# Regrouping the tokens of the expert stage from ragged per-batch blocks into one row of 1024-token blocks

## The chip, the cores and the metric

The kernel runs on one core of a Trainium2 chip. The metric is device time in microseconds (us) of one launch. The engines are PE (TensorE, matrix products), DVE (VectorE), ACT (ScalarE), POOL (GpSimd) and SP (SyncE, whose queue issues nearly all DMAs here). Each engine runs its own instructions strictly in program order and waits on semaphores for the others; the queue of SP does the same.

## The reference

There are 4 sequences of 3008 tokens. The first layer is a linear-algebra attention, the second a gated feed-forward block (called "experts" below) on all 12032 tokens:

```
scores = (z @ z^T) / S;  attn = max(scores, 0)**2;  x = u * (attn @ v)      # per sequence, S = 3008
xn = x / sqrt(mean(x*x) + 1e-6) * rms_g                                      # per token, 256 features
out = (silu(xn @ w_gate) * (xn @ w_val)) @ w_out                             # 256 -> 1536 -> 256
```

Each float32 operand is split into a high and a low part, and every product is three matmuls (high by high, high by low, low by high) of 128x128 weights on up to 512 columns.

## The kernel before

Attention works through the tokens of each sequence in three pairs of chunks: 1024, 1024 and 960 tokens. That makes 12 attention stages, A0 to A11, of 24 key blocks each. The expert layer takes the same 12 groups of tokens, M0 to M11: a group is cut in two halves of n columns (512, or 480 for the short third group of each sequence), and a seven-product scheme makes gate and value of both halves from seven split operands.

An expert stage runs 12 units (class Unit, one for each 128 hidden features). A unit issues 21 matmuls of n columns for the seven products and 12 more for the output product (`y`), 33 in all. Weights `wu` are loaded three units ahead. The program order is A0, A1, A2, M0, A3, M1, A4, M2, ... M8, A11, M9, M10, M11: the expert stage p comes right after attention stage p + 2.

Between attention and experts x goes through DRAM: `emit_gate` (L615) multiplies the attention result by u on DVE and writes it to a DRAM tile `xg`; it runs for the first chunk at the end of the first unit of the next expert stage and for the second chunk in its second unit, since the last three steps of an attention stage are carried over (`pend`). `load_x` (L626) fetches the 1024 or 960 columns back into `ux`; `norm_jobs` (L634) then makes 23 jobs of them: squares (ACT), add, transpose, reduce (DVE), all twice; one small matmul with `fold_sb` (L670) that sums over partitions; 13 tiny DVE instructions for the inverse root; two transposes back, four multiplications (L706) and four subtractions (L721). Seven split jobs (L753, L758) follow.

Where these jobs go is decided before anything is issued. `hook(phase, slot)` runs the jobs of a slot in the middle of the stage's own work; an expert unit f has the slots 3f, 3f + 1 and 3f + 2, so a stage has 36. The class Beside (L986) keeps a budget for every slot: 0.75 for DVE, and 1.35 for ACT in every third slot alone (slots 2, 5, ... 35). `put` goes through a list of jobs in order, gives each the first slot from the last one on that has room for its cost, and if no slot has room, the one with most room left from there on; the next job never goes to an earlier slot. In the stages M0, M3 and M6 `plan_batch` (L1057) puts the loads and splits of the next sequence's keys and values first: 18 casts of cost 0.6 on ACT. These three stages have one more particularity (`late_jobs`, L887): their slot 3f + 2 runs behind the unit's last DVE product and before its last three matmuls.

In this kernel the norm of group p stands in the following places. For p = 3, 6, 9 and for p = 5, 8 all of it lies beside expert stage M(p-1), with the load in the attention stage ahead. For p = 4, 7, 10 (`p % NP == 1`) the first 13 jobs are in attention stage A(p+1), and the other ten in M(p-1) from slot 1 on. The groups 0, 1, 2 and 11 have places of their own.

Of the kernel before, what the change touches and what calls it, by code (L numbers as in the profile page):

```python
# [8 lines left out]
F32 = mybir.dt.float32  # L9
# [10 lines left out]
P = 128  # L20
CH = 512
BLK = 32
# [8 lines left out]
def kernel(  # L31
# [13 lines left out]
    nc = tc.nc  # L45
    D, NT = uT.shape
# [3 lines left out]
    ND = D // P  # L50
    NF = DFF // P
    NK = -(-S // P)
    NC = -(-S // CH)
# [3 lines left out]
    NP = NC // 2  # L57
    PAIR = 2 * CH
    NPAIR = batch * NP
    NU = NF  # L60
    assert NC % 2 == 0 and NK % 4 == 0

    LA = 2
    LAG = 3
# [11 lines left out]
    dram = ctx.enter_context(tc.tile_pool(name="dram", bufs=1, space=bass.MemoryType.DRAM))  # L76

    def f32(ap):
        return ap.bitcast(F32)

    def where(p):

        b, j = divmod(p, NP)
        return b, 2 * j, b * S + j * PAIR, min(PAIR, S - j * PAIR)

    def width(c):
        return min(CH, S - c * CH)

    front = const.tile([P, FRONT], F32, name="front")
    woh = const.tile([P, NF, D], F32R, name="woh")  # L90
# [7 lines left out]
    def at(phase, slot, fn):  # L98
        jobs[phase, slot].append(fn)
# [182 lines left out]
    def prep_mov(p, k):  # L282
        b, c0, t0, n2 = where(p)
        c = c0 + k
        n = width(c)
        tiles = {}

# [32 lines left out]
    def prep_stat(b, c, shared=None):  # L320
        t0 = c * CH
        n = width(c)
        m = n + TAIL if n < CH else n
        lo = slice(DQK, P)
        tiles = shared if shared is not None else {}

        def load():
            raw = tiles["raw"] = new_raw("batch" if b else "start")
            nc.sync.dma_start(out=raw[:, :n], in_=zT2[:, b * S + t0:b * S + t0 + n])
            if n < m:  # L330
                nc.sync.dma_start(out=raw[:, n:m], in_=zT2[:, (b + 1) * S - TAIL:(b + 1) * S])

        def one():
            z = zst[b, c] = keep.tile([P, CH], F32R, tag=f"zst{c}", name=f"zst{c}")
            nc.scalar.copy(z[:, :m], tiles["raw"][:, :m])

        def two():
            raw, z = tiles["raw"], zst[b, c]
            nc.vector.tensor_tensor(z[lo, :m], raw[lo, :m], f32(z[lo, :m]), op=ALU.subtract)

        return load, one, two
# [255 lines left out]
    xg = {}  # L597
# [16 lines left out]

    def emit_gate(p, k):  # L615

        n = width(where(p)[1] + k)
        if p and p not in xg:
            xg[p] = dram.tile([ND, P, PAIR], F32, tag=f"xg{p}", name=f"xg{p}")
        for d in range(ND):  # L620
            x = us.pop((p, k, d))
            nc.vector.tensor_tensor(x[:, :n], acc[k, d][:, :n], x[:, :n], op=ALU.mult)
            if p:
                nc.sync.dma_start(out=xg[p][d, :, k * CH:k * CH + n], in_=x[:, :n])

    def load_x(p):  # L626
        n2 = where(p)[3]
        for d in range(ND):
            t = ux[p, d] = work.tile([P, PAIR], F32, tag=f"ux{d}", name=f"ux{d}")
            nc.sync.dma_start(out=t[:, :n2], in_=xg[p][d, :, :n2])  # L630
# [1 line left out]
    xsplit = {}  # L632

    def norm_jobs(p):  # L634
        n2 = where(p)[3]
        ns = [min(CH, n2 - k * CH) for k in range(2)]
        nb = n2 // BLK
        q = {}
# [1 line left out]
        m, y, w, pp = (small[:, k, :nb] for k in range(4))  # L640
        x = [ux[p, d] for d in range(ND)]
# [68 lines left out]
        n = n2 // 2  # L710
# [27 lines left out]
    ORDER = [A11, A12, S1, S2, S3, A22, S4]  # L738

    def split_jobs(p):  # L740
        n = where(p)[3] // 2
        last = p == NPAIR - 2

        def one(o):
            def high():
                val = xsplit[p, "values"][o]
                if last:
                    hi = keep.tile([P, CH], F32R, tag=f"vh{o}", name="xh")
                    lo = keep.tile([P, CH], F32R, tag=f"vl{o}", name="xl")
                else:  # L750
                    hi = moving.tile([P, CH], F32R, tag=f"xh{o}", name="xh")
                    lo = moving.tile([P, CH], F32R, tag=f"xl{o}", name="xl")
                nc.scalar.copy(hi[:, :n], val)  # L753
                xsplit[p, o] = (hi, lo)

            def low():
                hi, lo = xsplit[p, o]
                nc.vector.tensor_tensor(lo[:, :n], xsplit[p, "values"][o], f32(hi[:, :n]), op=ALU.subtract)  # L758

            return high, low  # L760

        return [one(o) for o in ORDER]
# [20 lines left out]
    class Unit:  # L783
        def __init__(self, p, f):
            self.p, self.f = p, f
            self.n = where(p)[3] // 2

        def product(self, ps, o, start, stop):
            wh, wl = units[self.p, self.f]
# [22 lines left out]
        def y(self, h):  # L812
            p, f, n = self.p, self.f, self.n
            if f == 0:
                for d in range(ND):
                    acc[h, d] = ps_a.tile([P, CH], F32, tag=f"acc{h}{d}", name="py")
            hi, lo = self.h[h]
            for d in range(ND):
                ds = slice(d * P, (d + 1) * P)
                nc.tensor.matmul(acc[h, d][:, :n], woh[:, f, ds], hi[:, :n], start=(f == 0), stop=False)  # L820
                nc.tensor.matmul(acc[h, d][:, :n], wol[:, f, ds], hi[:, :n], start=False, stop=False)  # L821
            for d in range(ND):
                ds = slice(d * P, (d + 1) * P)
                nc.tensor.matmul(acc[h, d][:, :n], woh[:, f, ds], lo[:, :n], start=False, stop=(f == NF - 1))  # L824
            if f == NF - 1:
                t0 = where(p)[2] + h * n
                for d in range(ND):
                    if p == NPAIR - 1 and h == d == 1:
                        out = work.tile([P, CH], F32, tag="T", name="y", bufs=6)
                    else:  # L830
                        out = work.tile([P, CH], F32, tag="out", name="y", bufs=3)
                    if d == 0:
                        nc.scalar.copy(out[:, :n], acc[h, d][:, :n])
                    else:
                        nc.vector.tensor_copy(out[:, :n], acc[h, d][:, :n])  # L835
                    nc.sync.dma_start(out=outT[d * P:(d + 1) * P, t0:t0 + n], in_=out[:, :n])
# [123 lines left out]
    def norms(p):  # L960
        if ("n", p) not in made:
            made["n", p] = norm_jobs(p)
        return made["n", p]
# [12 lines left out]
    def norm_plan(p):  # L976

        kinds = "addd addd tgggg ddd ddd dddd".replace(" ", "")
        cost = {"a": 1.3, "d": 0.7, "t": 0.0, "g": 0.7}
        out = []  # L980
        for i, k in enumerate(kinds):
            gap = 3 if i == 8 else 2 if i == 9 else 0
            out.append(("a" if k == "a" else "d", cost[k], gap, lambda i=i: whole(norms(p)[i])()))
        return out
# [24 lines left out]
    for p in range(NPAIR):  # L1009
        b, c0 = where(p)[:2]  # L1010
        ph = ("A", p)
        m = beside[p] = Beside(p)
# [33 lines left out]
    def plan_splits(p, phase, slots):  # L1046
        jobs_ = split_jobs_at(p)
        for (one, two), s in zip(jobs_, slots):
            at(phase, s, one)
            at(phase, s + 1 if s < NK - 1 else s, two)  # L1050

    def split_jobs_at(p):
        return [
            (lambda i=i: splits(p)[i][0](), lambda i=i: splits(p)[i][1]()) for i in range(NO)
        ]
# [29 lines left out]
    for i, (e, cost, gap, fn) in enumerate(norm_plan(0)):  # L1085
        g = 28 + i + (2 if i >= 8 else 0) if i < 13 else 48 + i - 13
        at(("A", g // NK), g % NK, fn)
    plan_splits(0, ("A", 2), range(17, 17 + NO))
    at(("A", 2), NK - 1, lambda: load_x(1))
    for p in range(1, NPAIR):  # L1090
        if p == 2:
            at(("M", 1), 0, lambda: load_x(2))
        elif 1 < p < NPAIR - 1:
            at(("A", p + 1), 8, lambda p=p: load_x(p))
        if p < NPAIR - 2:
            plan_splits(p, ("A", p + 2), range(16, 16 + NO) if p == 1 else range(NO))
        if p == 1:
            for i, (e, cost, gap, fn) in enumerate(norm_plan(1)[8:]):
                at(("A", 3), 1 + i, fn)
            continue  # L1100
        jobs_ = norm_plan(p)
        m = beside[p - 1]
        start = 1
        if p % NP == 1:
            early = 13
            for i, (e, cost, gap, fn) in enumerate(jobs_[:early]):
                at(("A", p + 1), 12 + i * 8 // early + (2 if i >= 8 else 0) + (1 if i >= 9 else 0), fn)
            jobs_ = jobs_[early:]
        elif p == 2:
            start = 4  # L1110
        elif p == NPAIR - 1:
            at(m.phase, 0, lambda p=p: load_x(p))
            start = 3
        h = m.put(jobs_, start)
        if p >= NPAIR - 2:
            for one, two in split_jobs_at(p):
                m.put([("a", 0.6, 0, one), ("d", 0.7, 0, two)], max(h, 15))

    for p in range(1, NPAIR):

        for k in range(2):
            load, split = prep_mov(p, k)[:2]
            if p >= LAG:
                m = beside[p - LAG]
# [123 lines left out]
```

## Time and profile before

| what | value |
|---|---|
| median of 3 runs | 2023.92 us (2022.46 to 2024.01) |
| span of the profiled execution | 2020.6 us; its own time is not recorded apart from the span |
| PE busy, weight loads busy | 2006.9 us (99%), 1675.6 us (83%) |
| DVE busy, ACT busy, POOL busy | 1604.6 us (79%), 1413.7 us (70%), 227.5 us (11%) |
| DMA | 328 MB, mean 163 GB/s |

Busy times of PE overlap from matmul to matmul, because a matmul's end is modelled; how fast PE really goes is read from the starts of two matmuls that follow each other. The profile's page also has the chain of work that ended last; the trace behind it answers with timelines, waits and groups by shape.

The stages stand in the trace of before at these times (first to last matmul of the seven products): M0 from 262.7 us, M1 from 439.3, M2 from 605.6, M3 from 758.9 to 848.2, M4 from 932.3, M6 from 1251.9 to 1341.2, M9 from 1745.6, M10 from 1835.8, M11 from 1925.8 to 2012.0.

### The profile page before, as it was taken

The page shows a single profiled execution, that of the slowest core. Times are in us where ns is not written, and L with a number is a line of the kernel's source. Part 1 is how long each engine was busy: PE and PEld are TensorE (multiplying, and loading weights), DVE is VectorE, ACT ScalarE, POOL GpSimd, SP SyncE. Part 2 cuts the span into 40 slices and gives each one's busy share as a digit, 9 for nine tenths or more (in the row PEclk, how much of TensorE's full clock was granted, in tenths as well). Part 3 has the DMA queues.
Part 4 walks back from the last instruction along what each step waited for, and adds up shares of the span by engine and source line. Part 5 has one row for each costly group of instructions (what it writes and reads, how often), then busy time and mean ns, then how long its engine had stood idle before and what let it go on. Part 6 is the DMA issues. An engine that isn't in the chain of part 4 may idle for free.

```text
span 2020.6 us, 27263 instructions
## 1 busy us (share of the span) xinstructions
PE 2006.9 (99%) x8976; PEld 1675.6 (83%) x8976; DVE 1604.6 (79%) x2693; ACT 1413.7 (70%) x2580; POOL 227.5 (11%) x376
## 2 busy tenths in 40 slices
PE   9999999999999999999999999999999999999999
PEld 7787878888888888888888888888888888888887
DVE  8989978987867768787786877888778777777765
ACT  8888867886765656796586665779658656566665
POOL 0547905000000001300000000320000000000000
PEclk9999999999999999999999999999999999999999
DMA  5135575373494697246348478625536747734342
GB/s 173 48 112 169 133 241 172 136 233 128 113 237 151 158 204 238 102 170 215 125 132 233 139 160 228 213 102 189 180 120 184 205 135 181 196 128 165 115 147 93
DMA packets 352367, 328.38 MB, mean 163 GB/s; under 512 B 221536, under 2 KB 268256, under 8 KB 352224
## 3 DMA queue, kind: packets, MB, share of 16 engines
q1 hardware_dynamic: 352224, 326.64, 53.6%
q8 instruction: 70, 1.15, 0.2%
q14 instruction: 73, 0.60, 0.1%
HBM read 189.73 MB, written 85.72 MB: 136 GB/s over the span
## 4 chain that ended last, share of the span: by engine, by line
PE 92%; DMA 2%; DVE 2%; issue 1%; POOL 1%; ACT 1%; SPq 0%; DVEq 0%; POOLq 0%; ACTq 0%
PE po L585 11%; PE po L586 11%; PE ps L793 11%; PE ps L792 11%; PE po L590 11%; PE ps L794 11%; PE py L820 6%; PE py L821 6%; PE py L824 6%; PE ps L457 4%; PE ps L456 4%; DMA wu<-wc 1%; POOL w L140 1%; POOL wolo L140 1%; DVE L L508 0%
## 5 line engine op out<-in xcount | busy, mean ns | idle before, releaser
L585 PE MATMUL po<-H,vh 128*128 128x512 f32 (+1 forms) x1152 | 446.7, 388 | 1.9 <-DVE y L835 1.0
L586 PE MATMUL po<-H,vl 128*128 128x512 f32 (+1 forms) x1152 | 445.0, 386 | 0.0
L799 ACT COPY s<-ps 128x512 f32<-128x512 f32 (+1 forms) x432 | 249.6, 578 | 215.2 <-PE ps L794 214.6
L793 PE MATMUL ps<-xh,wu 128*128 128x512 f32 (+1 forms) x1008 | 389.3, 386 | 1.7 <-DMA wu<-wc 1.6
L792 PE MATMUL ps<-xh,wu 128*128 128x512 f32 (+1 forms) x1008 | 390.0, 387 | 0.5 <-DMA wu<-wc 0.5
L794 PE MATMUL ps<-xl,wu 128*128 128x512 f32 (+1 forms) x1008 | 388.6, 386 | 0.0
L590 PE MATMUL po<-L,vh 128*128 128x512 f32 (+1 forms) x1104 | 336.5, 386 | 3.1 <-DVE L L508 2.9
L804 ACT CAST hH<-s 128x512 fp32r<-128x512 f32 (+1 forms) x288 | 176.6, 613 | 194.5 <-DVE s L891 187.5
L809 DVE TENSOR_TENSOR hL<-s,hH 128x512 fp32r<-128x512 f32 (+1 forms) x288 | 200.0, 694 | 100.0 <-ACT hH L804 88.6
L468 ACT ACTIVATE r<-ps 128x512 f32<-128x512 f32 x354 | 195.9, 595 | 105.3 <-PE ps L457 87.6
L585 PEld LDWEIGHTS po<-H,vh 128*128 128x128 f32 x1152 | 216.3, 188 | 45.9 <-ACT H L495 2.1
L586 PEld LDWEIGHTS po<-H,vl 128*128 128x128 f32 x1152 | 216.5, 188 | 39.8
L475 DVE TENSOR_TENSOR r<-ps,r 128x512 f32<-128x512 f32 (+1 forms) x287 | 186.5, 681 | 73.1 <-ACT r L468 72.3
L590 PEld LDWEIGHTS po<-L,vh 128*128 128x128 f32 x1104 | 206.5, 188 | 45.4 <-DVE L L508 6.5
L508 DVE TENSOR_TENSOR L<-r,H 128x512 fp32r<-128x512 f32 (+1 forms) x334 | 226.7, 712 | 9.7 <-ACT r L502 7.5
L820 PE MATMUL py<-hH,woh 128*128 128x512 f32 (+1 forms) x576 | 222.2, 386 | 0.1
L821 PE MATMUL py<-hH,wol 128*128 128x512 f32 (+1 forms) x576 | 222.0, 385 | 0.0
L793 PEld LDWEIGHTS ps<-xh,wu 128*128 128x128 f32 x1008 | 189.2, 188 | 38.8 <-DMA wu<-wc 3.7
L792 PEld LDWEIGHTS ps<-xh,wu 128*128 128x128 f32 x1008 | 189.2, 188 | 38.8 <-ACT s L799 1.9
L794 PEld LDWEIGHTS ps<-xl,wu 128*128 128x128 f32 x1008 | 189.2, 188 | 35.9
L370 POOL TENSOR_TENSOR vl<-raw,vh 128x128 fp32r<-128x128 f32 x144 | 78.8, 586 | 938.5 <-ACT vh L359 484.4
L824 PE MATMUL py<-hL,woh 128*128 128x512 f32 (+1 forms) x576 | 175.3, 385 | 0.0
(96 smaller groups left out, 2973.7 us busy)
## 6 DMA issues: line engine op xcount, KB each, us to landing
wu<-wc SPq DMA_DIRECT2D x288, 448.0 KB, 4.0
kept<-halves SPq DMA_DIRECT2D x168, 256.0 KB, 2.2
raw<-in_v SPq DMA_DIRECT2D x44, 256.0 KB, 3.5
raw<-in_zT SPq DMA_DIRECT2D x38, 256.0 KB, 4.5
u<-in_uT SPq DMA_DIRECT2D x36, 256.0 KB, 4.6
xg<-u SPq DMA_DIRECT2D x36, 256.0 KB, 2.2
out_T<-y SPq DMA_DIRECT2D x32, 256.0 KB, 2.0
ux<-xg SPq DMA_DIRECT2D x14, 512.0 KB, 4.4
```

Of the source, the lines that this page charges most:

```text
L508: nc.vector.tensor_tensor(lo[:, :n], a[:, :n], f32(hi[:, :n]), op=ALU.subtract)
L585: nc.tensor.matmul(po[d][:, :n], wh[:, j, ds], hi[:, :n], start=(i == 0), stop=False)
L586: nc.tensor.matmul(po[d][:, :n], wl[:, j, ds], hi[:, :n], start=False, stop=(ends and lo is None))
L590: nc.tensor.matmul(po[d][:, :n], wh[:, j, ds], lo[:, :n], start=False, stop=ends)
L792: nc.tensor.matmul(ps[:, :n], wh[:, o, :], xh[:, :n], start=start, stop=False, skip_group_check=True)
L793: nc.tensor.matmul(ps[:, :n], wl[:, o, :], xh[:, :n], start=False, stop=False, skip_group_check=True)
L794: nc.tensor.matmul(ps[:, :n], wh[:, o, :], xl[:, :n], start=False, stop=stop, skip_group_check=True)
L799: nc.scalar.copy(s, ps[:, :self.n])
L809: nc.vector.tensor_tensor(lo[:, :self.n], s, f32(self.h[h][0][:, :self.n]), op=ALU.subtract)
L820: nc.tensor.matmul(acc[h, d][:, :n], woh[:, f, ds], hi[:, :n], start=(f == 0), stop=False)
L821: nc.tensor.matmul(acc[h, d][:, :n], wol[:, f, ds], hi[:, :n], start=False, stop=False)
L824: nc.tensor.matmul(acc[h, d][:, :n], woh[:, f, ds], lo[:, :n], start=False, stop=(f == NF - 1))
```

## The change

The expert stages no longer follow the sequences: stage p takes the tokens 1024p to 1024p + 1023 of the whole row of 12032, and the last one the remaining 768. So stages M2, M5 and M8 have halves of 512 columns instead of 480, and M11 has halves of 384. The gate's output is written to whichever one or two `xg` tiles it belongs to. Stage p then needs the first 64, 128 or 192 columns of attention stage p + 1 too. For this reason the load of x and all 23 jobs of its norm go to M(p-1) for every p from 2 on: the load in slot 2, the jobs from slot 5 on (slots 0 and 3 for p = 11, as before). The part that placed 13 jobs of p = 4, 7, 10 in the attention stage ahead is gone.

```diff
+    def tokens(p):
+
+        return p * PAIR, min(PAIR, NT - p * PAIR)
...
     def emit_gate(p, k):
 
-        n = width(where(p)[1] + k)
-        if p and p not in xg:
-            xg[p] = dram.tile([ND, P, PAIR], F32, tag=f"xg{p}", name=f"xg{p}")
+        c0, t0 = where(p)[1:3]
+        n = width(c0 + k)
+        t0 += k * CH
         for d in range(ND):
             x = us.pop((p, k, d))
             nc.vector.tensor_tensor(x[:, :n], acc[k, d][:, :n], x[:, :n], op=ALU.mult)
-            if p:
-                nc.sync.dma_start(out=xg[p][d, :, k * CH:k * CH + n], in_=x[:, :n])
+            r = 0
+            while r < n and p:
+                m, off = divmod(t0 + r, PAIR)
+                e = min(n, r + PAIR - off)
+                if m not in xg:
+                    xg[m] = dram.tile([ND, P, PAIR], F32, tag=f"xg{m}", name=f"xg{m}")
+                nc.sync.dma_start(out=xg[m][d, :, off:off + e - r], in_=x[:, r:e])
+                r = e
...
     for p in range(1, NPAIR):
-        if p == 2:
-            at(("M", 1), 0, lambda: load_x(2))
-        elif 1 < p < NPAIR - 1:
-            at(("A", p + 1), 8, lambda p=p: load_x(p))
...
         jobs_ = norm_plan(p)
         m = beside[p - 1]
-        start = 1
-        if p % NP == 1:
-            early = 13
-            for i, (e, cost, gap, fn) in enumerate(jobs_[:early]):
-                at(("A", p + 1), 12 + i * 8 // early + (2 if i >= 8 else 0) + (1 if i >= 9 else 0), fn)
-            jobs_ = jobs_[early:]
-        elif p == 2:
-            start = 4
-        elif p == NPAIR - 1:
-            at(m.phase, 0, lambda p=p: load_x(p))
-            start = 3
+        at(m.phase, 0 if p == NPAIR - 1 else 2, lambda p=p: load_x(p))
+        start = 3 if p == NPAIR - 1 else 5
         h = m.put(jobs_, start)
```

`load_x`, `norm_jobs`, `split_jobs`, Unit and the output's address take their width and place from `tokens(p)` instead of `where(p)`. Line numbers of the changed file are 3 to 9 higher than those of before.

The first place is DVE at the end of expert stage M3, where the last unit ends and attention stage A6 begins. In the kernel before, with `hL` the low part for the output product, `s` the unit's values and `r` the attention scores, it reads:

```order
L309 SCALAR_TENSOR_TENSOR ml<-raw,mh 128x512
L809 TENSOR_TENSOR hL<-s,hH 128x512
L885 TENSOR_TENSOR s<-s 128x512
L891 TENSOR_TENSOR s<-ps,s 128x512
L844 TENSOR_TENSOR s<-ps,s 128x512
L809 TENSOR_TENSOR hL<-s,hH 128x512
L851 TENSOR_TENSOR s<-s 128x512
```

In the changed kernel the same place on DVE has these rows, shown in two pieces. The first starts at the unit's last product (L900, which was L891); `q` holds the squares of x of group 4, `misc` the sums:

```order
L900 TENSOR_TENSOR s<-ps,s 128x512
L673 TENSOR_REDUCE misc<-q_9034 128x16
L665 TENSOR_TENSOR q_9107<-q_9107,q_9108 128x512
L669 STREAM_TRANSPOSE q_9108<-q_9107 128x512
L673 TENSOR_REDUCE misc<-q_9108 128x16
L683 TENSOR_SCALAR misc<-ps 128x32
L686 TENSOR_SCALAR misc<-misc 128x32
L689 TENSOR_TENSOR misc<-misc 128x32
```

Ten more tiny instructions on `misc` follow, and then, still on DVE at the end of M3, the second piece up to the rows that stood there before:

```order
L708 STREAM_TRANSPOSE qt<-misc 128x512
L715 SCALAR_TENSOR_TENSOR ux_8258<-ux_8258,front,qt 128x512
L715 SCALAR_TENSOR_TENSOR ux_8260<-ux_8260,front,qt 128x512
L708 STREAM_TRANSPOSE qt<-misc 128x512
L715 SCALAR_TENSOR_TENSOR ux_8258<-ux_8258,front,qt 128x512
L715 SCALAR_TENSOR_TENSOR ux_8260<-ux_8260,front,qt 128x512
L730 TENSOR_TENSOR xc<-ux_8258 128x512
L730 TENSOR_TENSOR xc<-ux_8260,xc 128x512
L730 TENSOR_TENSOR ux_8258<-ux_8260,ux_8258 128x512
L730 TENSOR_TENSOR xc<-ux_8260,xc 128x512
L853 TENSOR_TENSOR s<-ps,s 128x512
L818 TENSOR_TENSOR hL<-s,hH 128x512
```

So 27 DVE instructions of group 4's norm now stand together between L900 and L853, which followed each other before; M6 has the same piece for group 7. On PE the matmul with `fold_sb` stands in the same place, between the unit's products A22 and S4:

```order
L803 MATMUL ps<-xl,wu 128x512
L679 MATMUL ps<-misc,fold_sb 128x32
L801 MATMUL ps<-xh,wu 128x512
L802 MATMUL ps<-xh,wu 128x512
L803 MATMUL ps<-xl,wu 128x512
L459 MATMUL ps<-mh,zst_8335 128x512
```

In the kernel before, no `fold_sb` matmul stands in M3 at all; it was in A5.

The second place is the queue of SP at the start of M1. In the kernel before:

```order
L630 DMA ux_5102<-xg_3201 128x960
L630 DMA ux_5104<-xg_3201 128x960
L624 DMA xg_5125<-u 128x512 x2
L776 DMA wu<-wc_80 128x896 x2
L624 DMA xg_5125<-u 128x512 x2
```

In the changed kernel, on the same queue at the start of M1:

```order
L632 DMA xg_3202<-u 128x64
L632 DMA xg_5123<-u 128x448
L632 DMA xg_3202<-u 128x64
L632 DMA xg_5123<-u 128x448
L639 DMA ux_5128<-xg_3202 128x1024
L639 DMA ux_5130<-xg_3202 128x1024
L785 DMA wu<-wc_80 128x896 x2
L632 DMA xg_5123<-u 128x512 x2
```

The load of x moved from ahead of the gate's writes to behind them, and reads a tile that two of these writes fill. The stages M2 to M9 have the same sequence, with first pieces of 64, 128 or 192 columns.

## Rows read from the trace of the kernel before

**Rows 1.** The profile's page: busy time of each engine, share of the span, instructions.
```profile
PE 2006.9 (99%) x8976; PEld 1675.6 (83%) x8976; DVE 1604.6 (79%) x2693; ACT 1413.7 (70%) x2580; POOL 227.5 (11%) x376
```

**Rows 2.** The profile's page: the chain that ended last, share of the span by engine.
```profile
PE 92%; DMA 2%; DVE 2%; issue 1%; POOL 1%; ACT 1%; SPq 0%; DVEq 0%; POOLq 0%; ACTq 0%
```

**Rows 3.** Waits of PE, longest in total: us, times, longest.
```profile
PE po L590 <- DVE L L508: 2.9, 4, 1.1
```

**Rows 4.** Timeline of PE at three widths: start, duration (us), engine, line, operation.
```profile
601.29 0.28 PE L456 MATMUL ps<-mh,zst 128*128 128x256 f32 x1
601.53 0.40 PE L585 MATMUL po<-H,vh 128*128 128x512 f32 x1
...
843.63 0.39 PE L820 MATMUL py<-hH,woh 128*128 128x512 f32 x1
847.71 0.39 PE L792 MATMUL ps<-xh,wu 128*128 128x512 f32 x1
...
2010.89 0.38 PE L792 MATMUL ps<-xh,wu 128*128 128x480 f32 x1
2014.36 0.60 PE L824 MATMUL py<-hL,woh 128*128 128x480 f32 x2
```

**Rows 5.** Weight loads by shape: count, busy us, mean ns, idle before.
```profile
L821 PEld LDWEIGHTS py<-hH,wol 128*128 128x128 f32 x576 | 108.1, 188 | 20.4
```

**Rows 6.** The norm's instructions by shape: count, busy us, mean ns, idle before.
```profile
L664 DVE TENSOR_REDUCE misc<-q 128x16 f32<-128x512 f32 x20 | 13.6, 678 | 0.1
L652 ACT ACTIVATE q<-ux 128x512 f32<-128x512 f32 x40 | 23.7, 629 | 8.4 <-DMA ux<-xg 5.6 <-DVE misc L664 1.5 <-DVE q L660 1.4
L656 DVE TENSOR_TENSOR q<-q,q 128x512 f32<-128x512 f32 x20 | 14.3, 713 | 7.5 <-ACT q L652 7.5
L660 DVE STREAM_TRANSPOSE q<-q 128x512 f32<-128x512 f32 x20 | 14.1, 704 | 0.1
L670 PE MATMUL ps<-misc,fold_sb 128*128 128x32 f32 x16 | 2.4, 232 | 0.0
L706 DVE SCALAR_TENSOR_TENSOR ux<-ux,front,qt 128x512 f32<-128x512 f32 x40 | 30.3, 759 | 0.0
L721 DVE TENSOR_TENSOR xc<-ux,xc 128x512 f32<-128x512 f32 x16 | 11.9, 741 | 0.0
```

**Rows 7.** Timeline of DVE: first and sixth of eight tiny instructions in a row.
```profile
757.17 0.19 DVE L680 TENSOR_TENSOR misc<-misc 128x32 f32<-128x32 f32 x1
758.28 0.19 DVE L691 TENSOR_TENSOR misc<-misc 128x32 f32<-128x32 f32 x1
```

**Rows 8.** Timeline at the end of M3, DVE and PE.
```profile
848.59 0.69 DVE L844 TENSOR_TENSOR s<-ps,s 128x512 f32<-128x512 f32 x1
849.36 0.69 DVE L809 TENSOR_TENSOR hL<-s,hH 128x512 fp32r<-128x512 f32 x1
851.56 0.62 PE L824 MATMUL py<-hL,woh 128*128 128x512 f32 x2
853.77 1.28 DVE L475 TENSOR_TENSOR r<-ps,r 128x512 f32<-128x512 f32 x2
```

**Rows 9.** Timeline of PE at the start of the span.
```profile
1.48 3.40 PE L124 MATMUL ps<-idle 128*128 128x512 f32 x8 [1.48 <-DVE idle L121]
```

**Rows 10.** A stretch after the last matmul: us; PE, PEld, DVE, ACT, POOL busy (count); granted clock; DMA.
```profile
2018.30:2020.60 2.30, 0.00 (x0) 0.00 (x0) 0.00 (x0) 0.00 (x0) 0.00 (x0) 0.50 0.38 146
```

**Rows 11.** Timelines of SP's queue and of ACT in M1.
```profile
446.21 0.92 SPq L624 DMA_DIRECT2D xg<-u  x2
...
452.82 1.14 ACT L652 ACTIVATE q<-ux 128x512 f32<-128x512 f32 x2
454.58 0.62 ACT L804 CAST hH<-s 128x512 fp32r<-128x512 f32 x1 [0.62 <-DVE s L891]
```

**Rows 12.** DMA issues: KB each, median us to landing; then the tile ux, minimum, median, maximum.
```profile
diag<-halves SPq DMA_DIRECT2D x8, 32.0 KB, 2.0
...
DMA to landing us min/median/max: 3.0/4.5/6.9
```

More of the change, by code (lines that the diff above doesn't have):

```diff
@@ L59 @@
     NPAIR = batch * NP
-    NU = NF
-    assert NC % 2 == 0 and NK % 4 == 0
+    assert NC % 2 == 0 and NK % 4 == 0 and -(-NT // PAIR) == NPAIR and NT % (2 * BLK) == 0
     LA = 2
@@ L622, in emit_gate @@
             nc.vector.tensor_tensor(x[:, :n], acc[k, d][:, :n], x[:, :n], op=ALU.mult)
-            if p:
-                nc.sync.dma_start(out=xg[p][d, :, k * CH:k * CH + n], in_=x[:, :n])
+            r = 0
[6 more added lines that the diff above has]
+                r = e
     def load_x(p):
-        n2 = where(p)[3]
+        n2 = tokens(p)[1]
         for d in range(ND):
@@ L634, in norm_jobs @@
     def norm_jobs(p):
-        n2 = where(p)[3]
+        n2 = tokens(p)[1]
         ns = [min(CH, n2 - k * CH) for k in range(2)]
@@ L740, in split_jobs @@
     def split_jobs(p):
-        n = where(p)[3] // 2
+        n = tokens(p)[1] // 2
         last = p == NPAIR - 2
@@ L785, in __init__ @@
             self.p, self.f = p, f
-            self.n = where(p)[3] // 2
+            self.n = tokens(p)[1] // 2
         def product(self, ps, o, start, stop):
@@ L825, in y @@
             if f == NF - 1:
-                t0 = where(p)[2] + h * n
+                t0 = tokens(p)[0] + h * n
                 for d in range(ND):
```

## The prediction

> **What bounds the kernel now.** I read the page first, then the waits of PE, then starts on PE's timeline. PE is busy 99% of the span and no other engine over 83% [rows 1]; 92% of the chain that ended last is PE itself [rows 2]; and the longest entry among PE's waits adds up to 2.9 us in the whole kernel [rows 3]. So the time is the number of matmuls times their spacing, and whatever makes PE wait is added to it nearly in full. The change keeps the matmuls: 33 in each of 12 units of 12 expert stages, 4752 before and after. It changes their widths, and it moves 23 norm jobs a group.
>
> The spacing at three widths comes from starts. In M3, 18 matmuls of 512 columns start between 843.63 and 847.71: 0.2267 us each. In M11, 16 of 480 columns between 2010.89 and 2014.36: 0.2169 us. Two of 256 columns take 0.24 us from 601.29 to 601.53: 0.12 us each [rows 4]. A narrow matmul is not cheaper in proportion: 480 columns are 94% of 512 and cost 96%.
>
> **Term 1, the widths.** Before, 4 stages of 396 matmuls have 480 columns: 1584 x 0.2169 = 343.6 us. After, three of these stages have 512 columns, 1188 x 0.2267 = 269.3 us, and M11 has 396 matmuls of 384 columns, a width that this trace doesn't hold. Bounds: in proportion to 512 columns, 0.170 us; carried on along the line from 512 to 480, 0.2169 - 3 x 0.0098 = 0.1875 us. The line between 256 and 480 columns gives 0.12 + 128/224 x 0.0969 = 0.1754, which is between two measured widths, so I take it: 69.5 us. The sum is 269.3 + 69.5 - 343.6 = -4.8 us, with ends of -7.0 and 0.0.
>
> A weight load is recorded with 188 ns [rows 5]. The Trainium skill ("TensorE: Matmul & The Clock Gate", section "LDWEIGHTS (loading the stationary operand)") gives the loading time as the number of weight columns divided by 1.2 in ns, 107 ns for 128 columns. If the recorded 188 ns were the floor of a matmul with its own load, 384 columns would cost 0.188 us and term 1 would be +0.1 us; by the rule the load stays hidden and the -4.8 stands. The pair of 256 columns at 0.12 us speaks for the rule.
>
> **Term 2, the norm at the end of M3 and M6.** This decides. `plan_batch` has put 18 casts of cost 0.6 into M3's ACT slots, two in each of 5, 8, ... 29. That leaves 0.15 of 1.35 in each; the norm's squares cost 1.3. Their first free slot is 32. The next two jobs go to 33 and 34, and since a job never goes to a slot ahead of the job before it, the first reduction, the second squares and all 18 jobs behind stand in slot 35, the last of the stage. The order shows it: 27 DVE instructions between L900 and L853, with one ACT pair and one PE matmul inside their chain. Before, 13 of the 23 jobs lay in A5 and ten in slots 1 to 16 of M3. M6 has the same for group 7. M9, beside which group 10's norm now lies, has no batch plan and stays spread out.
>
> The chain, with the durations of before [rows 6, 7]. First reduction 0.68; second square, which writes the tile that this reduction reads, 0.63; addition 0.71, transpose 0.70, reduction 0.68; matmul 0.23. Then 13 tiny instructions at 0.222 (five starts from 757.17 to 758.28 take 1.11): 2.89. Two transposes back, taken like the transpose at 0.70: 1.41; four multiplications at 0.759: 3.04; four subtractions at 0.741: 2.96. Sum 13.9 us.
>
> Before, L844 starts at 848.59, where the pile now starts, and the low part `hL` 0.77 later. Now L844's successor starts at 848.6 + 13.9 = 862.5, and `hL` ends at 862.5 + 0.77 + 0.69 = 864.0. The matmuls that need it (L824) started at 851.56 before [rows 8]. PE has other work until then: it first stops at the `fold_sb` matmul until the second reduction is done (about 4 us), then has 17 matmuls that wait for nothing from DVE, 3.9 us, and stops again. All of this lies ahead of 864.0, so the stage's end moves by 864.0 - 851.56 = 12.4 us. Behind `hL` on DVE stand the scores and low parts of A6's first blocks, all late by the same, so nothing is made good at once. Two stages: +24.8 us. Ends: wide DVE instructions overlap where one doesn't need the other (two take 1.28, not 1.36 [rows 8]), which takes 0.08 x 14 = 1.1 off, so 11.3; hops between engines, and the jobs of slots 33 and 34 in front, can add to about 14. So 22 to 28.
>
> What is saved where the 13 jobs left A5, A8 and A11: nothing, since PE waits there for none of them.
>
> **Term 3, the clock.** PE stands idle for two stretches of 4 to 7 us in each pile. Behind the last matmul of the kernel the granted clock is 0.50 [rows 10], the 1.2 GHz level. What a restart there costs shows at the start of the span: 8 matmuls of 512 columns take 3.40 us [rows 9], where 7 x 0.2267 + 0.39 = 1.98 would do at 2.4 GHz. So 1.4 us for the second stop of each pile (the first restart is hidden before the second stop): +2.8 us, between 0 and 6. The skill's page on TensorE's clock (same title, section "What's actually happening") has it that the low level is the default and activity lifts it, which is what these two rows look like; no row of before shows an idle stretch of this length in mid-kernel.
>
> **Term 4, the load of x behind the gate.** In M1, M2, M4, M5, M7, M8 and M9 the squares stand in slot 5 and the load in slot 2, right behind the gate's first chunk; it must wait for writes of two pieces. In M1 the first write is issued at 446.21, two take 0.92; squares ran at 452.82 for 1.14, and the next ACT instruction that PE needs at 454.58, 8.37 behind the first write [rows 11]. Now: third write issued at +0.92, landed 2.0 later (a 32 KB write; [rows 12]), +2.9; two load issues of about 0.46 and 4.5 us to land put the second half at +8.3, if both loads wait for the third write; +7.9 if the first needs only its own. Second square ends at +8.5 to 8.9: 0.15 to 0.5 us late, partly inside PE's queue of work. I take 0.15 x 7 = +1.0. The fastest landing of 3.0 makes it 0, the slowest of 6.9 up to 2.6 us a stage, 18 in all. Behind the waiting load on SP's queue stand weights for a unit three ahead (22 us away) and the gate's second writes, for which nobody waits in this stage.
>
> **Sum.** -4.8 + 24.8 + 2.8 + 1.0 = +23.8 us on a span of 2020.6: 2044.4. The median of the runs is 3.3 us above the profiled span, so 2047.7, say 2047.5.
>
> **Rivals.** (a) x lands late in the seven stages: ACT stops in program order, the copies out of PSUM behind it are late, and PE stops too. For it: before's squares already waited 5.6 us for x in all [rows 6]. Against: the median landing just makes it. At half of its upper end, 9 us instead of 1: about 2056. (b) The piles cost less: the wide instructions overlap, PE's clock stays up and PE wins a little back in A6, where DVE and ACT run ahead of it: -4.8 + 2 x 9.5 + 0 = +14, about 2038. For it: `hL` had 1.5 us to spare before L824. (c) The other side: the piles are hidden and the widths alone count, 2023.9 - 4.8 + 1.0 = 2020. This takes 13 us of PE work behind the product A22 that needs neither the pile nor what is queued behind it; the order has 17 matmuls, 3.9 us, and the first of the waits stands ahead of even these. It would only decide if 27 instructions ran in under 4 us.
>
> **Chances.** The forecast 0.78 (its own range 2041 to 2054), (a) 0.10, (b) 0.08, (c) 0.04. The range 2037 to 2058 takes in (b) and much of (a). About 0.2% is what a measurement of this kernel can tell from no change. Faster than that 0.03, within 0.01, slower 0.96.
>
> **What would show it.** In the changed profile: a wait of PE of about 4 us for a DVE row of `misc` at the `fold_sb` matmul and one of 6 to 8 us for `hL`, once each at the ends of M3 and M6; DVE without a gap there for 14 us; M11's matmuls 0.175 us apart; waits of ACT's squares for `ux` of a few tenths in seven stages. The prediction is wrong if PE's stop at the ends of M3 and M6 is under 8 us together in each, or if the total of the other waits grows by more than 8 us.

## The result and the profile after

The changed kernel takes 2045.09 us (median of 4 runs, 2044.0 to 2048.61) against 2023.97 us before (4 runs, 2022.46 to 2024.73): 1.0111 times, with a 95% interval of 1.0096 to 1.0125. The forecast was 2047.5 us. The profiled execution took 2044.17 us with a span of 2042.3 us, 21.7 more than before; that is what is taken apart here.

The page of the changed kernel, busy time of each engine, beside [rows 1]:

```profile
PE 2010.6 (98%) x8976; PEld 1676.7 (82%) x8976; DVE 1607.9 (79%) x2693; ACT 1413.0 (69%) x2580; POOL 226.7 (11%) x376
```

The instructions are the same in number and no engine is busy for more than 4 us longer. So the time is not new work, it is waiting. The waits of PE (us in total, times, longest) beside [rows 3] say for what:

```profile
PE py L833 <- DVE hL L818: 10.9, 2, 5.4
PE ps L679 <- DVE misc L673: 8.9, 2, 4.5
PE po L593 <- DVE L L511: 2.8, 4, 1.1
```

The third row stood at the top before. The two above it are new, come twice each, and make 19.8 us. Both lie at the ends of M3 and M6. DVE's timeline there (start, duration in us, line, operation; for M3, which now starts 1.98 us later than before):

```profile
850.13 0.68 DVE L900 TENSOR_TENSOR s<-ps,s 128x512 f32<-128x512 f32 x1
850.73 0.67 DVE L673 TENSOR_REDUCE misc<-q 128x16 f32<-128x512 f32 x1
852.10 0.69 DVE L665 TENSOR_TENSOR q<-q,q 128x512 f32<-128x512 f32 x1 [0.70 <-ACT q L661]
...
854.78 0.19 DVE L683 TENSOR_SCALAR misc<-ps 128x32 f32<-128x32 f32 x1 [0.52 <-PE ps L679]
...
857.70 0.71 DVE L708 STREAM_TRANSPOSE qt<-misc 128x512 f32<-128x512 f32 x1
...
863.78 0.68 DVE L730 TENSOR_TENSOR xc<-ux,xc 128x512 f32<-128x512 f32 x1
864.38 0.68 DVE L853 TENSOR_TENSOR s<-ps,s 128x512 f32<-128x512 f32 x1
864.98 0.68 DVE L818 TENSOR_TENSOR hL<-s,hH 128x512 fp32r<-128x512 f32 x1
```

Between L900 and L853, which followed each other directly in [rows 8], stand 27 instructions of group 4's norm, and they take 13.65 us from 850.73 to 864.38. DVE stops only twice, for 0.70 and 0.52 us, in a chain that goes over to ACT and PE and back. PE's timeline at the same place:

```profile
854.31 0.43 PE L679 MATMUL ps<-misc,fold_sb 128*128 128x32 f32 x2 [4.46 <-DVE misc L673]
854.56 0.77 PE L801 MATMUL ps<-xh,wu 128*128 128x512 f32 x1
855.13 0.63 PE L802 MATMUL ps<-xh,wu 128*128 128x512 f32 x1
855.55 0.63 PE L803 MATMUL ps<-xl,wu 128*128 128x512 f32 x1
...
859.90 0.39 PE L830 MATMUL py<-hH,wol 128*128 128x512 f32 x1
865.72 1.22 PE L833 MATMUL py<-hL,woh 128*128 128x512 f32 x2 [5.43 <-DVE hL L818]
866.74 0.63 PE L459 MATMUL ps<-mh,zst 128*128 128x512 f32 x1
867.17 0.63 PE L460 MATMUL ps<-ml,zst 128*128 128x512 f32 x1
...
871.76 0.39 PE L459 MATMUL ps<-mh,zst 128*128 128x512 f32 x1
...
949.38 0.39 PE L801 MATMUL ps<-xh,wu 128*128 128x512 f32 x1
```

First the stop for the sums, then 17 matmuls that need nothing from DVE, then the stop for `hL`, whose end on DVE (864.98 + 0.68) is the moment at which PE goes on. Behind each stop starts lie about 0.43 us apart instead of 0.2267, and a matmul is shown with 0.63 us; the last row is the first matmul of M4. The granted clock beside it (stretch; its length; PE, PEld, DVE, ACT, POOL busy with counts; granted clock; DMA):

```profile
849.80:852.00 2.20, 0.05 (x1) 0.00 (x0) 1.60 (x3) 1.06 (x3) 0.00 (x0) 1.00 0.02 4
852.00:854.30 2.30, 0.00 (x0) 0.00 (x0) 2.09 (x3) 0.57 (x2) 0.00 (x0) 1.00 0.00 0
854.40:857.50 3.10, 3.10 (x9) 2.52 (x10) 2.31 (x13) 0.00 (x0) 0.00 (x0) 0.53 0.00 0
...
863.00:865.70 2.70, 0.00 (x0) 0.00 (x0) 2.66 (x5) 0.60 (x2) 0.00 (x0) 0.83 0.00 0
865.80:871.60 5.80, 5.80 (x14) 4.54 (x15) 5.72 (x10) 4.60 (x9) 0.00 (x0) 0.50 0.23 90
872.00:880.00 8.00, 8.00 (x37) 6.60 (x36) 7.15 (x14) 7.90 (x14) 0.00 (x0) 1.00 0.46 169
```

While PE stands idle the clock still reads 1.00 at first; the matmuls behind the stop run at 0.50, the 1.2 GHz level. Behind the second stop 14 of them start in the 6.04 us from 865.72 to 871.76, where 14 x 0.2267 = 3.17 us would do at 2.4 GHz.

At last the width that no row of before held. M11 on PE's timeline, with 22 matmuls between these two rows:

```profile
1989.78 0.33 PE L802 MATMUL ps<-xh,wu 128*128 128x384 f32 x1
...
1993.77 0.33 PE L801 MATMUL ps<-xh,wu 128*128 128x384 f32 x1
```

That is 23 starts in 3.99 us, 0.1735 us each.

The account by stages, where a stage runs from its first to its last matmul with `wu` and an attention stretch from there to the next stage. M2, M5 and M8 grew from 86.28, 86.33 and 86.15 to 89.81, 89.90 and 89.81 us, +10.8 in all; M11 shrank from 86.15 to 69.87, -16.3. M3 with A6 takes 188.5 us instead of 173.4, M6 with A9 188.6 instead of 173.5: +30.2. M0 is 1.8 shorter, the end behind M11's last such matmul 0.9 shorter. This makes +22.0 of the 21.7; the rest is in stretches that differ by some tenths each.

### The profile page after: what moved, and what is told of

Its sections match the earlier page's. It is cut to its first block, busy times and chain, and to the rows that moved or that the text cites. A ratio compares the mean times of both kernels' runs of the same rounds, so it can differ in the third digit from the quotient of the medians.

```text
span 2042.3 us, 27270 instructions
## 1 busy us (share of the span) xinstructions
PE 2010.6 (98%) x8976; PEld 1676.7 (82%) x8976; DVE 1607.9 (79%) x2693; ACT 1413.0 (69%) x2580; POOL 226.7 (11%) x376
## 5 line engine op out<-in xcount | busy, mean ns | idle before, releaser
L833 PE MATMUL py<-hL,woh 128*128 128x512 f32 (+1 forms) x576 | 176.9, 388 | 10.9 <-DVE hL L818 10.9
```

## The experiments

The theory: the two piles of 27 instructions, which stand on DVE ahead of what PE needs next, cost some 27 to 30 us, and the widths give back 5.5. The rivals: the wider stages or the moved load of x cost it, or the piles are only where a lack of DVE time shows that would be there anyway. Except in the first, the edit is made in the changed kernel, or in that of experiment 2 where the text says so.

**1. The pile alone, in the kernel before.** All 23 jobs of groups 4 and 7 go into M3 and M6, with the old widths and the old load of x:

```diff
-        if p % NP == 1:
+        if p in (4, 7):
+            start = 5
+        elif p % NP == 1:
             early = 13
```

> The kernel before, with its old groups of 1024, 1024 and 960 tokens and x loaded in the attention stage ahead as before, but with all 23 norm jobs of groups 4 and 7 handed to M3 and M6 behind the batch plan, so that 20 of them land in slot 35. Theory (the pile alone makes the change slow): two stops of PE of 4.5 and 5.5 us in each of M3 and M6 and 2.7 us at the low clock behind the second, 2 x 15 = +30 us on 2024, so about 2054 us (ratio 1.015). Rival (the new token blocks, the narrow last block or the load of x behind the gate cost the time): about 2024 us.

Measured: 2051.37 us (2050.93 to 2051.97) against 2022.32 us for the kernel before on the same chip, 1.0141 times (1.0126 to 1.0157). Its waits of PE:

```profile
PE py L824 <- DVE hL L809: 10.0, 2, 5.4
PE ps L670 <- DVE misc L664: 8.9, 2, 4.5
```

The same two rows, the first 0.9 us shorter in all, without a changed width and without a moved load. So the pile costs 29 us by itself. The whole change costs 21 to 22, so the rest of it gives 7 to 8 back. The rival that laid the time to widths and load falls.

**2. The pile taken away.** The planner is told that the squares of groups 4 and 7 cost 0.1 instead of 1.3, so they find room beside the casts in early slots, and the 21 jobs behind them follow at their places. The work is the same:

```diff
+        if p in (4, 7):
+            jobs_ = [(e, 0.1 if e == "a" else cost, gap, fn) for e, cost, gap, fn in jobs_]
         h = m.put(jobs_, start)
```

> The changed kernel, with the squares of groups 4 and 7 entered in the plan at a cost of 0.1 instead of 1.3, so that they share slots 5 and 14 of M3 and M6 with two casts each and the other jobs spread over slots 8 to 35, none in a heap. Theory (pile): the 30 us go and the widths' gain of about 5 us is left: 2015 us, ratio 0.9955 to before; the crowded ACT slots cost under 1 us. Rival (blocks or load of x cost the time): stays near 2045 us.

Measured: 2021.54 us (11 runs, 2020.68 to 2024.83), 0.9997 times the kernel before (0.9989 to 1.0006). Its span of 2020.7 us is 21.6 below that of the changed kernel. The longest waits of PE now, apart from one for `L` as in [rows 3]:

```profile
PE ps L802 <- DMA wu<-wc: 1.8, 3, 0.7
PE po L588 <- DVE y L844: 1.5, 4, 0.5
PE ps L801 <- ACT s L808: 1.4, 4, 0.4
```

Both rows of the pile are gone, with the same work on DVE, so it was the order and not a lack of DVE time. The 2015 us expected were too low by 6.5. Beside the kernel before, M3 is 1.4 and M6 2.3 us longer (90.71 and 91.64 us), and A6, A7 and A9 0.7 each; M5 and M8 are 1.0 longer than in the changed kernel. That is 7.8 us in waits of some tenths, for squares that stand ahead of copies on ACT, for copies of `y` on DVE, for weights that land late: they eat what the widths give.

**3. Work for PE during the idle stretch.** To keep the clock up, 20 matmuls whose results nobody reads stand behind the `fold_sb` matmul, writing other columns of the same PSUM tile:

```diff
+            if p in (4, 7):
+                any_ = woh[:, 0:2, :].rearrange("p a d -> p (a d)")
+                for _ in range(20):
+                    nc.tensor.matmul(ps[:, 64:], woh[:, 0, :P], any_[:, 64:], start=True, stop=True)
```

> The changed kernel with 20 extra matmuls of 448 columns behind the fold matmul of groups 4 and 7; they write columns of the same PSUM tile that nobody reads and give PE about 5 us of work inside the time in which it waits for the pile. Theory (5 to 6 us of the 30 are the clock that fell while PE stood idle): the second stop shrinks to about 1 us, the granted clock stays at 1.0 behind it, and the time falls by 2 x 2.7 = 5 us to about 2040. Rival (the slow matmuls behind the stop were DVE and ACT being late, not the clock): stays at 2045, or rises if the extra matmuls are in the way.

Measured: 2058.69 us, 1.0178 times the kernel before (1.0164 to 1.0192); by the spans 12.9 us longer than without the extra work (2055.2 to 2042.3). Its longest wait of PE, two stretches of M3's end with the columns as above, and a row of DVE's timeline:

```profile
PE py L837 <- DVE hL L822: 14.2, 2, 7.1
```

```profile
854.00:858.00 4.00, 3.05 (x9) 2.79 (x10) 0.86 (x2) 0.00 (x0) 0.00 (x0) 0.50 0.01 2
858.00:862.00 4.00, 4.00 (x16) 3.58 (x16) 0.08 (x1) 0.00 (x0) 0.00 (x0) 0.73 0.00 0
```

```profile
861.92 0.19 DVE L687 TENSOR_SCALAR misc<-ps 128x32 f32<-128x32 f32 x1 [7.02 <-PE ps L684]
```

The experiment failed to test what it was meant to. DVE did nearly nothing until about 862: the instruction that reads the 32 columns of the sums waited until the extra matmuls into the other columns of the tile were done, so the whole rest of the pile started about 6 us later and PE's second stop grew to 7.1 us. The fill had made the chain itself longer. The trace says what DVE waited for: in the changed kernel the `fold_sb` matmul raises the semaphore that this instruction waits for; here only the last of the 20 extra matmuls does, at 861.88. So it is a wait of the program, which signals once for the whole tile.

**4. The same fill behind the reads.** 16 such matmuls, issued behind DVE's two instructions of `guess` instead of ahead of them. Only the first of the two reads the sums in PSUM (the expectation says both do); the second works on what the first wrote. The edit, shown against the changed kernel:

```diff
-            q["ps"] = ps[:, :nb]
+            q["tile"], q["ps"] = ps, ps[:, :nb]
...
         def cubic():
+            if p in (4, 7):
+                any_ = woh[:, 0:2, :].rearrange("p a d -> p (a d)")
+                for _ in range(16):
+                    nc.tensor.matmul(q["tile"][:, 64:], woh[:, 0, :P], any_[:, 64:], start=True, stop=True)
```

> As e3_fill, with 16 extra matmuls of 448 columns that write unread columns of the same PSUM tile, but issued behind the two DVE instructions that read this tile, so that DVE's pile does not wait for them. In e3_fill the first of these waited for the last extra matmul, some 6 us in each stage, which is where its +13 us came from. Theory (the clock costs 2.7 us behind the second stop): the pile ends when it did, the second stop shrinks from 5.5 to about 1.5 us, the granted clock stays near 1.0 behind it, and the time is 2045 - 5 to 6 = 2039 to 2040 us. Rival (the slow stretch is DVE and ACT being late): 2045 us.

Measured: 2043.8 us (2042.82 to 2045.76), 1.0109 times the kernel before (1.0093 to 1.0124), which can't be told from the changed kernel. The 2039 to 2040 us of the theory did not come, and by the time alone the rival's 2045 is the nearer. Two of its waits, a stretch behind PE's second stop and two matmuls in it say more:

```profile
PE py L837 <- DVE hL L822: 2.6, 2, 1.8
PE po L588 <- DVE y L848: 2.5, 4, 0.8
```

```profile
866.00:869.00 3.00, 2.17 (x10) 1.53 (x9) 2.81 (x5) 2.35 (x5) 0.00 (x0) 1.00 0.00 0
```

```profile
867.56 0.39 PE L459 MATMUL ps<-mh,zst 128*128 128x512 f32 x1
867.79 0.40 PE L460 MATMUL ps<-ml,zst 128*128 128x512 f32 x1
```

The second stop shrank from 10.9 to 2.6 us in all, because PE had been given something to do, and the clock stays at 1.00 behind it. The matmuls there start 0.23 us apart although DVE is as late as before, so the slow stretch of the changed kernel was the clock, and the rival falls by the trace. M3 with A6 takes 186.9 us instead of 188.5, M6 with A9 186.7 instead of 188.6. So with the clock up 1.6 and 1.9 us come back of the 2.9 and 3.0 that the slow matmuls behind each second stop take; the rest, 1.1 us a stage and 0.2 by which M3's pile ended later here, is lost again, mostly at waits for DVE's copies of `y`, as DVE is late anyway. In the changed kernel PE has no such waits there. The idle stop itself costs nothing that a busy PE would win back: PE can't go on before `hL`.

**5. Half of the pile.** The kernel of experiment 2, but the last ten jobs of groups 4 and 7 (the two transposes back, four multiplications, four subtractions) are put into the stage's last slot:

```diff
-        h = m.put(jobs_, start)
+        h = m.put(jobs_[:13] if p in (4, 7) else jobs_, start)
+        if p in (4, 7):
+            for _, _, _, fn in jobs_[13:]:
+                at(m.phase, 3 * NF - 1, fn)
```

> As e4_squares_beside, but the last ten norm jobs of groups 4 and 7 (two transposes back, four multiplications, four subtractions, all DVE) stand in slot 35 of M3 and M6, the first 13 spread out; so a heap of ten without PE or ACT in its chain. Theory (a heap costs PE its length less the 1.5 us that the low part had to spare, and the clock falls only behind a long stop): these ten took 6.7 us in the changed kernel (857.70 to 864.38), the low part ends 6.7 us late, PE waits 5.2 us once in each stage: e4's 2021.5 + 10.4 = 2032 us, up to 2036 if the clock falls behind it. Rival (most of the loss is the first stop at the fold matmul and the hops between the engines): under 2 us a stage, 2025 us or less.

Measured: 2032.78 us (2031.67 to 2034.25), 1.0054 times the kernel before (1.004 to 1.0067); its span of 2030.9 us is 10.2 above that of experiment 2. One wait of PE is left of the two, and the clock behind it:

```profile
PE py L833 <- DVE hL L818: 9.8, 2, 4.9
```

```profile
860.70:865.70 5.00, 5.00 (x12) 3.94 (x13) 4.92 (x9) 4.03 (x8) 0.00 (x0) 0.51 0.19 74
```

Ten instructions of 6.7 us make PE stop for 4.9 us, where 5.2 were expected from 6.7 less the 1.5 that `hL` was early by. So the price of a pile grows with its length and begins as soon as the slack is used up. That the sum met the forecast is partly luck: M3 with A6 is 6.8 us and M6 with A9 6.0 us longer than in experiment 2, as the clock fell too, and small waits that experiment 2 has in other stages, M5 and A7 above all, are missing here.

**6. The margin of the load of x.** The kernel of experiment 2, with the jobs of the norm from slot 2 on instead of 5, right behind the load, in the seven stages M1, M2, M4, M5, M7, M8 and M9:

```diff
-        start = 3 if p == NPAIR - 1 else 5
+        start = 3 if p == NPAIR - 1 else 5 if p in (4, 7) else 2
```

> As e4_squares_beside, but the squares of the groups 2, 3, 5, 6, 8, 9 and 10 start in slot 2, right behind the load of x, instead of slot 5. Theory (slot 5 is just late enough for x to have landed about 8 us behind the gate's first write): ACT waits about 7 us for x in seven stages and PE for ACT's copies about 6 us each, with some clock on top: 2015 + 45 to 55 = 2060 to 2070 us. Rival (the load would be hidden anyway): as e4_squares_beside, 2015 us.

Measured: 2081.22 us (2 runs), 1.029 times the kernel before (1.0271 to 1.0308). The wait of PE, then the wait of ACT behind which it stands:

```profile
PE ps L801 <- ACT s L808: 45.3, 11, 6.7
```

```profile
ACT q L661 <- DMA ux<-xg: 53.8, 16, 7.4
```

This is rival (a) of the prediction, made to happen: the squares wait for x on ACT, the copy out of PSUM stands behind them in ACT's order, and PE stands behind the copy. Each of the seven stages is 6.7 to 9.7 us longer than in experiment 2, 57 us in all. The time is 11 us above the upper end of what was expected: 6.5 of them are the base of 2015 us, where experiment 2 measured 2021.5. Of the 57 us 44 are PE's waits beyond those of experiment 2; the other 13 would be the low clock, whose mean was 0.987 where experiment 2 has 1.000, and for which the expectation had put only "some". That split was not tried apart. In the changed kernel three slots lie between, and ACT's squares wait for x 1.1 us in all.

**7. The norm planned ahead of the casts.** The first 8 jobs of groups 4 and 7 get their slots before the 18 casts do, the rest before the seventh cast; the casts' cost is 0.45 there, so that three fit where two did:

```diff
+            if b > 1 and k == 0:
+                m.put(norm_plan((b - 1) * NP + 1)[:8], 5)
+            if b > 1 and k == NC:
+                m.put(norm_plan((b - 1) * NP + 1)[8:], 11)
...
-            h = m.put([("a", 0.6, 0, one), ("d", 0.7 if dve else 0.0, 0, two)], s + (4 if k < 2 else 2))
+            h = m.put([("a", 0.45 if b > 1 else 0.6, 0, one), ("d", 0.7 if dve else 0.0, 0, two)], s + (4 if k < 2 else 2))
...
+        if p in (4, 7):
+            continue
```

> The changed kernel with another plan for M3 and M6: the first eight norm jobs of groups 4 and 7 are put first (squares in slots 5 and 8, alone there), the 18 casts of the batch plan follow three to a slot (cost 0.45) in slots 11 to 26, and the other 15 norm jobs behind the first six casts, up to slot 31. Theory (what was left in e4_squares_beside, about 5 us more waits of PE in M3, A6, M6 and A9, is the crowding of squares and two casts in one ACT slot and of the plan's end): M3 and M6 wait for under 0.7 us each and the time is 2021.5 - 4 = 2017 us, ratio 0.9975. Rival (the batch plan and a whole norm do not fit beside one expert stage, whatever their order): 2021 us, as e4_squares_beside.

Measured: 2019.89 us (11 runs, 2017.68 to 2021.83) against 2022.06 us before (15 runs), 0.9988 times (0.9979 to 0.9997). The interval lies just below 1: faster than the kernel before, by some 2 us. The 2017 us expected were too low by 3, and M3 and M6 did not come under 0.7 us. From experiment 2 (0.9997 times the kernel before, 0.9989 to 1.0006), and so from the rival's 2021 us, it can hardly be told, as the two intervals overlap. Its longest wait of PE, again apart from that for `L`:

```profile
PE ps L801 <- ACT s L808: 2.3, 5, 0.9
```

A6 and A9 lose nothing now beside the kernel before, M3 and M6 still 2.0 and 2.5 us, M9 1.4. So the change's own gain, 5.5 us by the widths, comes out by less than half even with the norm spread out. M3 and M6 have to hold a whole norm beside their 18 casts, where they held ten of its jobs; that this is what they lose by was not tried apart.

## Why the prediction was right

**What bounds the kernel.** Right: PE is busy for 98%, and what makes it wait shows in the time nearly in full.

**Term 1, the widths.** Taken at -4.8 us, measured -5.5 by the stages' lengths. The step by the line between two measured widths gave 0.1754 us for 384 columns, and 0.1735 was measured: 396 of them make 0.75 us, which is the difference. The other end, the line from 512 to 480 carried on, was off by 0.014 us, the proportional one by 0.0035. The 188 ns recorded for a weight load are no floor: matmuls with their own loads start 0.1735 us apart here. The 107 ns by the Trainium skill's rule ("TensorE: Matmul & The Clock Gate", section "LDWEIGHTS (loading the stationary operand)") fit under that.

**Term 2, the piles.** Taken at 12.4 us each. The first matmul with `hL` behind the pile starts at 865.72, before at 851.56 [rows 8]; with M3's later start of 1.98 us taken off this is 12.2 us. The chain, summed up row by row from [rows 6, 7], was to take 13.9 and took 13.65. DVE was not without a gap there, as the prediction had it: it stood for 0.70 us until the second squares were done and for 0.52 until the `fold_sb` matmul was, where the chain had 0.63 and 0.23. PE's first stop was put at 4 us and is 4.46. The second was put at 6 to 8 and is 5.43, since the 17 matmuls ahead of it ran in part at 1.2 GHz and filled more of the stretch; the moment at which PE goes on is set by DVE, so nothing of that is in the time.

**Term 3, the clock.** This is the term that was mis-sized: 1.4 us for the second stop of each pile, by the 8 matmuls of the kernel's start [rows 9]. Behind the stop in mid-kernel 14 matmuls of M3 took 6.04 us where 3.17 would do, 2.9 us, and those of M6 lost 3.0, twice what was forecast. All of it is in the time: from the first matmul with `hL` behind the pile to the first one of M4 PE takes 83.66 us (865.72 to 949.38), before it took 80.76 (851.56 [rows 8] to 932.32), and between M6 and M7 it is 83.76 instead of 80.76. No wait of PE but that for `hL` stands in these stretches. That the first restart is hidden before the second stop was right. The start of the kernel gave the right mechanism and too small a number of slow matmuls. The number isn't fixed either: behind the same pile in experiment 1 the same stretches are only 1.5 and 2.2 us longer than before.

The trace now shows the low level in mid-kernel too: 0.50 under the matmuls behind the stop, then 1.00 behind 871.76. The Trainium skill's page on TensorE's clock ("TensorE: Matmul & The Clock Gate", section "What's actually happening") has it that activity lifts the clock from a low level, and the trace agrees.

Together M3 with A6 and M6 with A9 grew by 30.2 where terms 2 and 3 had 27.6. The piles make 12.2 + 12.1 = 24.3 and the clock 2.9 + 3.0 = 5.9, which is all of it.

**Term 4, the load of x.** Taken at +1.0, measured about 0. The tile `ux` in the changed kernel, wait of its squares and the landings, beside [rows 12]:

```profile
  DMA ux<-xg: 1.1, 2
...
DMA to landing us min/median/max: 2.9/4.5/7.0
```

The landings are as before and two squares wait, not some in each of seven stages; no wait of PE comes from it. The estimate put the second half of x at 7.9 to 8.3 us behind the first write and the next ACT instruction that PE needs at 8.37; the margin is small but it held. Experiment 6 shows what lay behind it: rival (a), some 8 us a stage once the squares come three slots earlier.

**What was not foreseen.** M0 is 1.8 us shorter; PE's waits for weights there fell from 1.6 to 0.3 us. In experiment 1, whose order in M0 is that of before, it is 0.9 shorter, so part of this wanders from run to run, and its cause was not tried. The kernel's end is 0.9 us shorter with narrower last blocks. By the terms the sum is -5.5 + 24.3 + 5.9 - 1.8 - 0.9 - 0.3 = 21.7, with the 0.3 for all the rest. So that the forecast of +23.8 came within about 2 us is partly luck: the clock was 3.1 us too small in it, and the gains at M0 and at the end, the widths and the load of x made up for that and more. The pile, which decides, was within 0.5 us. The forecast then added 3.3 us from the span to the median of the runs; for the changed kernel that step is 2.8.

**The rivals.** (b), cheaper piles at 2038, fell: wide instructions overlapped by 0.08 us each (863.78 to 864.38 is 0.60 for a duration of 0.68) and saved 0.25 us of the 13.9, and the clock cost more, not less. (a), a late x, did not come, as term 4 shows. (c), piles hidden, fell by experiment 1, which shows them alone at 29 us.

## What to carry to other kernels

When a planner puts jobs into slots in order and runs out of room, look at the last slot: whatever stands there in a heap is paid at its full length less the slack of what comes next, on an engine that works in order (13.65 us of DVE made PE 12.2 us late, 6.7 made it 5.0 late). The matmuls that run at the low clock behind the stop come on top, 1.5 to 3.0 us a stop here. The busy share of the engine says nothing against that: DVE was at 79% with the piles and without them. And an idle TensorE is only worth filling if something behind it can start earlier; filler ahead of a chain's own reads makes the chain longer.

## What was not expected of the hardware

The granted clock fell late. It read 1.00 all through the first idle stretch of 4.46 us, and 0.50 only under the matmuls that followed. In the second idle stretch it fell before PE went on (0.83 in the mean of 863.00 to 865.70). It stayed low for different stretches: until 858.06 behind the first stop, which is 3.5 us of matmuls, and until 871.76 behind the second, which is 6.0 us. What decides between the two no run shows.

The wait of DVE in experiment 3 looks like one of these surprises and isn't one: by the semaphores in its trace it is the program's own wait, and no run here shows whether the chip would have let the read go ahead of the matmuls into other columns.

A matmul of 384 columns costs 77% of one of 512 (0.1735 to 0.2267 us), and one of 480 costs 96% [rows 4]: 384 is 75% of the width, 480 is 94%, so both widths pay nearly in proportion. M11, which had 480 columns before, has a fifth fewer and is 19% shorter.
